# Softmax sums in fewer matmuls: two steps' exponentials added on VectorE, the last keys' products and sums in quarters of the array, sums' transfers on other queues

## The chip, the cores and the metric

The kernel runs on one core of a Trainium2 chip. The metric is the device time of one execution in microseconds (us). Three runs of the kernel before took 581.74, 581.37 and 588.43 us, a median of 581.74 us.

## The reference

Attention with capped scores over 24 heads (2 batches of 12), 448 queries and 448 keys a head, head dimension 64, followed by two feed-forward layers on the 896 x 768 result. All is float32.

```
scores = cap * tanh((q @ k.T / 8) / cap)
attn   = exp(scores - max) / (sum(exp(scores - max)) + 1e-9)
x      = attn @ v                                # 24 x 448 x 64 -> 896 x 768
h      = x @ w_in1;  y = (h * cos(h)) @ w_out1   # 768 -> 2048 -> 768
h      = y @ w_in2;  o = (h * sigmoid(h)) @ w_out2
```

The kernel leaves out the maximum (the cap bounds the scores), and divides after the product with v.

## The kernel before, in words

**The attention stage** works on pairs of heads, p = 0 to 11. The 448 keys of a head are three full chunks of 128 and a rest of 64. One pair's exponentials are the tile e32 of [128 keys, 7, 448 queries]: chunk 2t+u is step t of head u, and chunk 6 holds the two rests, head 0 in partitions 0 to 63 and head 1 in 64 to 127.

- `S_pe` makes the transposed scores of a step: for t = 0 to 2 with three matmuls a head on rounded high and low parts (float32r), head 0 on rows 0 to 63 of the array and head 1 on rows 64 to 127; step 3 in plain float32, two matmuls of 64 columns each. `S_tanh` and `S_exp` on ScalarE follow.
- `PV` multiplies with v into the bank po: rows 0 to 63 of po are head 0, 64 to 127 head 1. A matmul has all 128 keys and 64 columns, so two stand side by side in the array. For the rests v is padded with zeros to 128 keys. These are 8 matmuls a pair.
- `PV_sums` multiplies a block of ones with each chunk into the bank sm, in four column quarters of 32 (two quarters a head, to be added later): 8 matmuls a pair. A float32 matmul shows as two records in the trace.
- `evac`, `evac_sums` (VectorE) copy po and sm out. Four small transfers on SP's queue spread the rows of sums over 32 partitions, `recip` adds the two quarters and inverts, a transfer to DRAM (rs) and two back (rb) broadcast the result, `norm_mul` and `norm_split` make the high and low part of x.

The order on every engine is that of the program text (a manual schedule). Turn p of the loop issues the scores, tanh and exponentials of pair p+1, then `recip` of p-2, `qk_split` of p+2 (high and low parts of q and k), a few steps that prepare the first three weight blocks (the table `early`: w_guard and w_hi on ScalarE, w_floor, w_bits and w_lo on VectorE, w_load on POOL's queue), normalisation of p-3, the products and the sums of p and their copies. The banks po and sm are single. In the last turn the sums stand ahead of the products. The queue of SP carries vf (the loads of v), sums, rs and rb; POOL's queue carries raw (q and k, from pair 3 on) and some weights.

**The layers behind it** are matmuls against weights that are split on the way (lines 486 to 606). The first, `gemm_in`, begins with two column blocks on batch 0 (36 matmuls), four of six row blocks of batch 1 (24), and then the last two row blocks of batch 1 (24), which are pairs 10 and 11.

Of the kernel before, what the change touches and what calls it, by code (L numbers as in the profile page):

```python
# [28 lines left out]
F32 = mybir.dt.float32  # L29
# [4 lines left out]
ALU = mybir.AluOpType  # L34
# [3 lines left out]
def tile_attention_ffn_ffn(  # L38
# [10 lines left out]
    nc = tc.nc  # L49
    B, H, S, D = shape  # L50
    DM = out.shape[1]
    DFF = w_in1.shape[0] * 128
    P = 128
# [10 lines left out]
    const = ctx.enter_context(tc.tile_pool(name="const", bufs=1))  # L64
# [94 lines left out]
    with ExitStack() as actx:  # L159
        dpool = actx.enter_context(tc.tile_pool(name="dr", bufs=2, space=bass.MemoryType.DRAM))  # L160
        ap_ = actx.enter_context(tc.tile_pool(name="att", bufs=2))
        ps_s = actx.enter_context(tc.tile_pool(name="ps_s", bufs=3, space=PSUM))
        ps_o = actx.enter_context(tc.tile_pool(name="ps_o", bufs=1, space=PSUM))
        NPT = NHEAD // 2
        NCH = 7
        NV = NCH + 1
# [11 lines left out]
        ones = const.tile([P, 3, Q], F32, name="ones")  # L178

        def v_init():  # L180
            nc.gpsimd.memset(ones[:, 0], 1.0)
            for u in range(2):
                for h in range(2):
                    nc.gpsimd.memset(ones[h * D:(h + 1) * D, 1 + u], float(u == h))

# [14 lines left out]
        def load_v(p):  # L200
            if p >= NPT:
                return
            vf[p] = ap_.tile([P, NV, D], F32, tag="vf", name=f"vf{p}", bufs=2)
            nc.sync.dma_start(vf[p].rearrange("p c d -> p (c d)"), qkv[p][:, PAD + QK:])

        qh, ql = {}, {}

        def qk_split(p, part=slice(0, FULL)):
            if p >= NPT:
                return  # L210
            if p not in qh:
# [39 lines left out]

        po_, sm_ = {}, {}


        def PV(p, steps):
            first = p not in po_
            if first:
                po_[p] = ps_o.tile([P, 512], F32, tag="po", name=f"po{p}")[:, :S]
            for n, t in enumerate(steps):
                for c in range(0, P, W):  # L260
                    u, f = divmod(c, D)
                    nc.tensor.matmul(po_[p][c:c + W], vf[p][:, 2 * t + u, f:f + W], e32[p][:, min(2 * t + u, NCH - 1), :],  # L262
                                     start=first and n == 0, stop=t == 3)


        def PV_sums(p, steps):
            first = p not in sm_
            if first:
                sm_[p] = ps_o.tile([P, 512], F32, tag="sm", name=f"sm{p}")[:, :S]
            for n, t in enumerate(steps):  # L270
                for c in range(4):
                    u, x = divmod(c, 2)
                    chunk = 4 * t + 2 * x + u
                    one = ones[:, 0] if chunk < NCH - 1 else ones[:, 1 + u]
                    nc.tensor.matmul(sm_[p][c * Q:(c + 1) * Q], one, e32[p][:, min(chunk, NCH - 1), :], start=first and n == 0, stop=t == 1)  # L275

        xu, sums, rb = {}, {}, {}

        def evac(p):
            xu[p] = ap2.tile([P, S], F32, tag="xu", name=f"xu{p}", bufs=4)  # L280
            nc.vector.tensor_copy(xu[p], po_.pop(p))

        def evac_sums(p):
            x = ap2.tile([P, S], F32, tag="xs", name=f"xs{p}", bufs=2)
            sums[p] = ap2.tile([32, 2, S // 16], F32, tag="sums", name=f"sums{p}", bufs=2)
            nc.vector.tensor_copy(x[:3 * Q + 1], sm_.pop(p)[:3 * Q + 1])
            for u in range(2):
                for y in range(2):
                    at = u * D + y * Q
                    nc.sync.dma_start(sums[p][16 * u:16 * u + 16, y], x[at:at + 1])  # L290

        def recip(p):
            if p < 0:
                return
            s = sums.pop(p)
            nc.vector.tensor_tensor(out=s[:, 0], in0=s[:, 0], in1=s[:, 1], op=ALU.add)
            nc.vector.reciprocal(out=s[:, 0], in_=s[:, 0])
            d = dpool.tile([2, S], F32, tag="rs", name=f"rs{p}")
            nc.sync.dma_start(d.rearrange("h (a n) -> (h a) n", a=16), s[:, 0])
            r = ap2.tile([P, S], F32, tag="rb", name=f"rb{p}", bufs=4)  # L300
            for u in range(2):
                nc.sync.dma_start(r[u * D:(u + 1) * D, :], d[u:u + 1].to_broadcast([D, S]))  # L302
# [18 lines left out]
        def warm_up(n, ps):  # L321
            for _ in range(n):
                nc.tensor.matmul(ps, zero[:, :P], zero, start=True, stop=True)


        early = {}
        for w, turn in ((0, 2), (1, 4), (2, 6)):
            for at, *step in ((0, w_guard, w, None), (1, w_floor, w, nc.vector), (1, w_bits, w, 0), (2, w_bits, w, 1), (2, w_bits, w, 2),
                              (2, w_load, w + 2, nc.gpsimd), (3, w_hi, w), (4, w_lo, w)):
                early.setdefault(turn + at, []).append(step)  # L330
        early.setdefault(NPT - 2, []).append((w_guard, 3, None))
        early.setdefault(NPT - 1, []).append((w_floor, 3, nc.gpsimd))
# [20 lines left out]
                S_exp(0, slice(0, 4))  # L353
        S_exp(0, slice(4, NCH))
        qk_split(1)
        warm_up(4, ps_o.tile([P, 512], F32, tag="sm", name="warm1")[:, :S])
        PV(0, [0, 1])
        PV_sums(0, [0])
        for p in range(NPT):
            load(p + 3)  # L360
            if p > 0:
                load_v(p + 1)
            for t in range(3):
                S_pe(p + 1, t)
                S_tanh(p + 1, t)
            S_pe(p + 1, 3)
            S_tanh(p + 1, 3)
            S_exp(p + 1)
            recip(p - 2)
            qk_split(p + 2)  # L370
            for f, *a in early.get(p, []):
                f(*a)
            if p == NPT - 1:
                recip(p - 1)
            norm_mul(p - 3)
            norm_split(p - 3)
            if p == NPT - 1:
                PV_sums(p, [0, 1])
# [272 lines left out]
```

## Time and profile before

| | |
|---|---|
| Median of three runs | 581.74 us |
| Profiled execution, its own time | 580.33 us |
| Its span, first to last instruction | 578.5 us |
| TensorE busy | 567.1 us (98%) |
| VectorE, ScalarE, GpSimd busy | 379.9, 265.1, 155.7 us |
| Granted TensorE clock, mean | 0.997 |

The span is what lies between the first and the last instruction; the execution's time has 1.8 us around it. PE is TensorE's matmuls, DVE VectorE, ACT ScalarE, POOL GpSimd, SP the engine that only issues transfers. An L with a number is a line of the kernel before. A matmul's shown duration includes its way through the array, so that the start of one to the start of the next says what it costs. "[0.70 <-ACT e L244]" behind a row is the time that the engine stood idle ahead of it, and who ended that.

### The profile page before, as it was taken

What the parts mean: (1) busy time and instruction counts of PE and PEld (TensorE: products, weight loads), DVE (VectorE), ACT (ScalarE), POOL (GpSimd) and SP (SyncE); (2) the same over time, 40 slices, a digit from 0 to 9 for tenths busy, and PEclk for the clock granted to TensorE, in tenths of its full rate; (3) what the DMA queues carried; (4) which work ended last, traced back from release to release, by engine and by line L of the source; (5) the groups of instructions that cost most, each with busy time, mean ns of one, the idle gap of its engine ahead of it and who ended that gap; (6) DMA issues with size and microseconds to landing.
All of it is one profiled execution on the core that took longest, in us unless ns stands there. A gap on an engine that the chain in (4) does not pass through costs nothing.

```text
span 578.5 us, 7770 instructions
## 1 busy us (share of the span) xinstructions
PE 567.1 (98%) x3060; PEld 486.7 (84%) x3060; DVE 379.9 (66%) x490; ACT 265.1 (46%) x307; POOL 155.7 (27%) x84
## 2 busy tenths in 40 slices
PE   8999999889999999999999999999999999999997
PEld 4444443779999999999999999999999999999997
DVE  3356885489998888667646552888877866644501
ACT  6989985167777766233323222433333323232201
POOL 1001101033444433242332221344222223313300
PEclk9999999989999999999999999999999999999999
DMA  7245642123333323343433330343333334443102
GB/s 282 88 123 175 185 133 71 48 78 104 132 126 109 110 92 101 101 145 93 134 110 108 109 127 30 114 148 121 109 110 109 110 110 137 136 141 121 53 1 95
DMA packets 18755, 65.51 MB, mean 113 GB/s; under 512 B 4192, under 2 KB 7776, under 8 KB 18720
## 3 DMA queue, kind: packets, MB, share of 16 engines
q1 hardware_dynamic: 17280, 57.95, 31.1%
q0 software_dynamic: 1152, 6.78, 3.4%
q8 instruction: 24, 0.39, 0.3%
q10 hardware_dynamic: 288, 0.30, 0.2%
q14 instruction: 11, 0.09, 0.0%
HBM read 62.14 MB, written 2.80 MB: 112 GB/s over the span
## 4 chain that ended last, share of the span: by engine, by line
PE 88%; DMA 6%; DVE 2%; ACT 2%; SPq 1%; issue 0%; DVEq 0%
PE h L419 38%; PE o L566 20%; PE y L419 20%; PE po L262 4%; PE sc L232 2%; DMA rs<-sums 2%; DMA rb<-rs 2%; PE sm L275 2%; PE sc L236 1%; ACT e L244 1%; ACT e L250 1%; DMA raw<-in_qkv 1%; SPq L290 1%; SPq L302 1%; DMA sums<-xs 0%
## 5 line engine op out<-in xcount | busy, mean ns | idle before, releaser
L120 POOL TENSOR_SCALAR w<-w 128x768 f32<-128x768 f32 (+1 forms) x63 | 148.2, 2352 | 315.5 <-ACT w L114 251.4
L419 PE MATMUL h<-x,whi 128*128 128x448 f32 x768 | 219.6, 367 | 3.9 <-DVE x L315 3.7
L419 PEld LDWEIGHTS h<-x,whi 128*128 128x128 f32 x768 | 145.0, 189 | 16.9 <-DVE x L315 4.0
L419 PE MATMUL h<-x,wlo 128*128 128x448 f32 x384 | 140.9, 367 | 0.0
L144 ACT ACTIVATE whi<-w 128x768 fp32r<-128x768 f32 (+1 forms) x66 | 54.3, 823 | 144.0 <-DVE w L136 133.4
L566 PE MATMUL o<-whi,g 128*128 128x384 f32 x448 | 114.3, 335 | 0.0
L419 PE MATMUL y<-g,whi 128*128 128x448 f32 x384 | 109.2, 366 | 0.0
L133 DVE SCALAR_TENSOR_TENSOR w<-w,wraw 128x768 int32<-128x768 int32 (+1 forms) x66 | 61.6, 933 | 43.5 <-POOL w L120 42.5
L151 DVE TENSOR_TENSOR wlo<-w,whi 128x768 fp32r<-128x768 f32 (+1 forms) x66 | 61.4, 931 | 31.7 <-ACT whi L144 30.9
L566 PEld LDWEIGHTS o<-whi,g 128*128 128x128 f32 x448 | 81.0, 188 | 0.0
L419 PEld LDWEIGHTS h<-x,wlo 128*128 128x128 f32 x384 | 72.6, 189 | 5.7
L419 PEld LDWEIGHTS y<-g,whi 128*128 128x128 f32 x384 | 72.1, 188 | 5.9
L566 PE MATMUL o<-wlo,g 128*128 128x384 f32 x224 | 75.1, 335 | 0.0
L419 PE MATMUL y<-g,wlo 128*128 128x448 f32 x192 | 70.2, 366 | 0.0
L136 DVE SCALAR_TENSOR_TENSOR w<-wraw,w 128x768 uint32<-128x768 uint32 (+1 forms) x66 | 61.6, 934 | 2.3
L131 DVE TENSOR_SCALAR wraw<-wraw 128x768 int32<-128x768 int32 (+1 forms) x66 | 56.0, 849 | 9.7 <-ACT w L114 9.7
L114 ACT ACTIVATE w<-wraw 128x768 f32<-128x768 f32 (+1 forms) x66 | 58.0, 879 | 3.4 <-DMA wraw<-in_moe_w_out 3.4
L244 ACT ACTIVATE e<-sc,scap 128x896 f32<-128x896 f32 (+1 forms) x48 | 40.0, 913 | 12.1 <-PE sc L232 12.1
L566 PEld LDWEIGHTS o<-wlo,g 128*128 128x128 f32 x224 | 42.0, 188 | 0.0
L475 ACT ACTIVATE r<-h 128x896 f32<-128x896 f32 (+1 forms) x18 | 14.8, 835 | 58.7 <-PE h L419 56.8
L262 PE MATMUL po<-e,vf 128*64 128x448 f32 x192 | 38.5, 541 | 0.7 <-ACT e L250 0.5
L419 PEld LDWEIGHTS y<-g,wlo 128*128 128x128 f32 x192 | 36.1, 188 | 3.0
(54 smaller groups left out, 398.4 us busy)
## 6 DMA issues: line engine op xcount, KB each, us to landing
wraw<-in_moe_w_in SPq DMA_DIRECT2D x29, 768.0 KB, 4.3
wraw<-in_moe_w_out SPq DMA_DIRECT2D x22, 768.0 KB, 4.3
wraw<-in_moe_w_out SPq DMA_DIRECT2D x12, 640.0 KB, 4.0
raw<-in_qkv POOLq DMA_DIRECT2D x9, 480.0 KB, 4.5
vf<-in_qkv SPq DMA_DIRECT2D x12, 256.0 KB, 3.3
rb<-rs SPq DMA_DIRECT2D x24, 112.0 KB, 2.9
out<-os SPq DMA_DIRECT2D x13, 192.0 KB, 1.9
wraw<-in_moe_w_in POOLq DMA_DIRECT2D x3, 768.0 KB, 5.2
```

Of the source, the lines that this page charges most:

```text
L114: nc.scalar.activation(out=w32[i][:, :n, :].bitcast(F32), in_=wraw[i][:, :n, :, 1].bitcast(F32), func=AF.Abs, scale=2.0 ** -48)
L120: eng.tensor_scalar(out=t, in0=t, scalar1=2.0 ** -63, scalar2=None, op0=ALU.max)
L131: nc.vector.tensor_scalar(out=w1, in0=w1, scalar1=-0x80000000, scalar2=None, op0=ALU.bitwise_and)
L133: nc.vector.scalar_tensor_tensor(out=t, in0=t, scalar=3, in1=w1, op0=ALU.logical_shift_left, op1=ALU.bitwise_or)
L136: nc.vector.scalar_tensor_tensor(out=t, in0=w0.bitcast(U32), scalar=29, in1=t, op0=ALU.logical_shift_right, op1=ALU.bitwise_or)
L144: nc.scalar.activation(out=whi[i][:, :n, :], in_=w32[i][:, :n, :].bitcast(F32), func=AF.Copy)
L151: nc.vector.tensor_tensor(out=wlo[i][:, :n, :], in0=w32.pop(i)[:, :n, :].bitcast(F32), in1=whi[i][:, :n, :].bitcast(F32), op=ALU.subtract)
L244: nc.scalar.activation(out=e32[p][:, 2 * t:2 * t + n, :], in_=sc.pop((p, t))[:, :n, :S], func=AF.Tanh, scale=scap)
L262: nc.tensor.matmul(po_[p][c:c + W], vf[p][:, 2 * t + u, f:f + W], e32[p][:, min(2 * t + u, NCH - 1), :], start=first and n == 0, stop=t == 3)
L419: nc.tensor.matmul(pt, l, r, start=first and m == 0, stop=last and m == len(ops) - 1)
L475: nc.scalar.activation(out=r, in_=h, func=AF.Silu)
L566: nc.tensor.matmul(pt[t], l, r[:, cols], start=k == 0 and m == 0, stop=k == KF - 1 and m == 2)
```

## The change

Six matmuls of `PV` (steps 0 to 2) stay as they are. The rests, step 3, go to a new function `PV_mixed`: four matmuls of 64 keys by 64 columns, each in a quarter of the array, two of them products into po, two of them sums into sm, so v needs no padding. `PV_sums` keeps four matmuls of 32 columns: VectorE first adds the exponentials of step 0 and step 1 of both heads (`e_add`, [128, 2, 448]), and these two blocks and the two of step 2 are summed. The heads' sums now lie crosswise in sm, which rb puts right. The sums go out in two transfers on POOL's queue, v from pair 2 on too; for the last pair sums, rs and rb are on ScalarE's queue. In the last turn `recip(10)` stands behind the products, the last pair's sm lies in a bank pair of the scores, and the steps of `early` are spread over one more turn.

```diff
-            vf[p] = ap_.tile([P, NV, D], F32, tag="vf", name=f"vf{p}", bufs=2)
-            nc.sync.dma_start(vf[p].rearrange("p c d -> p (c d)"), qkv[p][:, PAD + QK:])
+            vf[p] = ap_.tile([P, NCH, D], F32, tag="vf", name=f"vf{p}", bufs=2)
+            (nc.gpsimd if p > 1 else nc.sync).dma_start(vf[p].rearrange("p c d -> p (c d)"), qkv[p][:, PAD + QK:])
...
+        def acc(d, p, tag):
+            if p in d:
+                return d[p], False
+            t = ps_o.tile([P, 512], F32, tag=tag, name=f"{tag}{p}") if p < NPT - 1 or tag == "po" else ps_s.tile([P, 2, 512], F32, tag="sc", name=f"{tag}{p}")[:, 0]
+            d[p] = t[:, :S]
+            return d[p], True
...
+        def PV(p, steps, last=False):
+            po, first = acc(po_, p, "po")
             for n, t in enumerate(steps):
...
+                for u in range(2):
+                    nc.tensor.matmul(po[u * D:(u + 1) * D], vf[p][:, 2 * t + u, :], e32[p][:, 2 * t + u, :],
+                                     start=first and n == 0, stop=last and n == len(steps) - 1)
...
+        def PV_mixed(p, last=False):
+            po, first = acc(po_, p, "po")
+            sm, _ = acc(sm_, p, "sm")
+            for u in range(2):
+                rows, other = slice(u * D, (u + 1) * D), slice((1 - u) * D, (2 - u) * D)
+                e = e32[p][rows, NCH - 1, :]
+                nc.tensor.matmul(po[rows], vf[p][rows, NCH - 1, :], e, start=first, stop=last)
+                nc.tensor.matmul(sm[other], ones[rows, Q:], e, start=True, stop=False)
...
+        def PV_sums(p):
+            sm, _ = acc(sm_, p, "sm")
+            x = e01.pop(p)
+            for c, e in enumerate((x[:, 1], e32[p][:, 5, :], x[:, 0], e32[p][:, 4, :])):
+                nc.tensor.matmul(sm[c * Q:(c + 1) * Q], ones[:, :Q], e, start=False, stop=True)
...
+        def e_add(p):
+            if p >= NPT:
+                return
+            e01[p] = ap_.tile([P, 2, S], F32, tag="e01", name=f"e01_{p}", bufs=2)
+            nc.vector.tensor_tensor(out=e01[p], in0=e32[p][:, 0:2, :], in1=e32[p][:, 2:4, :], op=ALU.add)
...
-            for u in range(2):
-                for y in range(2):
-                    at = u * D + y * Q
-                    nc.sync.dma_start(sums[p][16 * u:16 * u + 16, y], x[at:at + 1])
+            for y in range(2):
+                (nc.gpsimd if p < NPT - 1 else nc.scalar).dma_start(sums[p][:, y], x[y * Q:y * Q + D + 1:D])
...
+            eng = nc.sync if p < NPT - 1 else nc.scalar
+            eng.dma_start(d.rearrange("h (a n) -> (h a) n", a=16), s[:, 0])
...
+                eng.dma_start(r[u * D:(u + 1) * D, :], d[1 - u:2 - u].to_broadcast([D, S]))
...
-        for w, turn in ((0, 2), (1, 4), (2, 6)):
-            for at, *step in ((0, w_guard, w, None), (1, w_floor, w, nc.vector), (1, w_bits, w, 0), (2, w_bits, w, 1), (2, w_bits, w, 2),
-                              (2, w_load, w + 2, nc.gpsimd), (3, w_hi, w), (4, w_lo, w)):
+        for w, turn in ((0, 1), (1, 4), (2, 6)):
+            for at, *step in ((0, w_guard, w, None), (1, w_floor, w, nc.vector), (1, w_bits, w, 0), (2, w_bits, w, 1), (3, w_bits, w, 2),
+                              (3, w_load, w + 2, nc.gpsimd), (4, w_hi, w), (5, w_lo, w)):
...
+        e_add(0)
         warm_up(4, ps_o.tile([P, 512], F32, tag="sm", name="warm1")[:, :S])
         PV(0, [0, 1])
-        PV_sums(0, [0])
...
             recip(p - 2)
+            if p > 0:
+                e_add(p)
             qk_split(p + 2)
...
-            if p == NPT - 1:
-                recip(p - 1)
             norm_mul(p - 3)
             norm_split(p - 3)
...
+            if p < NPT - 1:
+                PV(p, [0, 1, 2] if p else [2])
+                PV_mixed(p, True)
+                evac(p)
+                PV_sums(p)
                 evac_sums(p)
-            PV(p, range(4) if p else [2, 3])
-            evac(p)
-            if p < NPT - 1:
-                PV_sums(p, [0, 1] if p else [1])
+            else:
+                PV_mixed(p)
+                PV_sums(p)
                 evac_sums(p)
+                PV(p, [0, 1, 2], True)
+                evac(p)
+        recip(NPT - 2)
```

What TensorE has from the last scores of pair 2 to the first of pair 3, before (po1 and sm1 are the banks of pair 1, xN the count of equal instructions; each float32 one shows as two records):

```order
L232 MATMUL sc2_2_260<-qh2_218,ql2_219 128x448 x2
L236 MATMUL sc2_3_268<-raw2_128 64x448 x2
L262 MATMUL po1_277<-e32_1_195,vf1_130 64x448 x8
L275 MATMUL sm1_288<-e32_1_195,ones_94 32x448 x8
L232 MATMUL sc3_0_308<-qh3_273 128x448 x2
```

and with the change (its own line numbers: 263 is `PV`, 273 and 274 `PV_mixed`, 281 `PV_sums`):

```order
L233 MATMUL sc2_3_263<-raw2_125 64x448 x2
L263 MATMUL po1_276<-e32_1_189,vf1_127 64x448 x6
L273 MATMUL po1_276<-e32_1_189,vf1_127 64x448
L274 MATMUL sm1_283<-e32_1_189,ones_94 64x448
L273 MATMUL po1_276<-e32_1_189,vf1_127 64x448
L274 MATMUL sm1_283<-e32_1_189,ones_94 64x448
L281 MATMUL sm1_283<-e01_1_268,ones_94 32x448
L281 MATMUL sm1_283<-e32_1_189,ones_94 32x448
L281 MATMUL sm1_283<-e01_1_268,ones_94 32x448
L281 MATMUL sm1_283<-e32_1_189,ones_94 32x448
L229 MATMUL sc3_0_303<-qh3_270 128x448 x2
```

Sixteen matmuls behind the scores have become fourteen: two and eight of the old ones are gone, four of 64 x 64 and four of 32 columns have come.

VectorE in the last turn, before (xu, xs are the copies of po and sm, L296 and L297 are `recip`, L308 `norm_mul`):

```order
L281 COPY xu10_988<-po10_979 128x448
L286 COPY xs10_999<-sm10_990 97x448
L296 TENSOR_TENSOR sums9_927<-sums9_927 32x28
L297 RECIPROCAL sums9_927<-sums9_927 32x28
L296 TENSOR_TENSOR sums10_1000<-sums10_1000 32x28
L297 RECIPROCAL sums10_1000<-sums10_1000 32x28
L308 TENSOR_TENSOR rb8_969<-xu8_840,rb8_969 128x448
L315 CAST x2_1_73<-rb8_969 128x448
L316 TENSOR_TENSOR x2_1_73<-rb8_969,x2_1_73 128x448
L286 COPY xs11_1033<-sm11_1024 97x448
```

and with the change:

```order
L300 COPY xs10_974<-sm10_963 97x448
L308 TENSOR_TENSOR sums9_904<-sums9_904 32x28
L309 RECIPROCAL sums9_904<-sums9_904 32x28
L289 TENSOR_TENSOR e01_11_986<-e32_11_917 128x896
L151 TENSOR_TENSOR wlo2_988<-w32_2_650,whi2_949 128x768
L321 TENSOR_TENSOR rb8_944<-xu8_821,rb8_944 128x448
L328 CAST x2_1_73<-rb8_944 128x448
L329 TENSOR_TENSOR x2_1_73<-rb8_944,x2_1_73 128x448
L300 COPY xs11_1004<-sm11_995 97x448
L295 COPY xu11_1015<-po11_994 128x448
L308 TENSOR_TENSOR sums10_975<-sums10_975 32x28
L309 RECIPROCAL sums10_975<-sums10_975 32x28
```

The reciprocal of pair 10 has moved from ahead of the copy xs of pair 11 to behind it; the sum e01 of pair 11 and a weight's step stand ahead of that copy.

SP's queue in turns 3 and 4, before:

```order
L290 DMA sums3_449<-xs3_448 16x1x28 x4
L204 DMA vf5_457<-in_qkv 128x512
L299 DMA rs2_491<-sums2_372 32x28
L302 DMA rb2_493<-rs2_491 64x448 x2
L290 DMA sums4_530<-xs4_529 16x1x28 x4
```

and POOL's queue in turns 3 and 4 with the change:

```order
L201 DMA vf4_373<-in_qkv 128x448
L302 DMA sums3_441<-xs3_440 32x1x28 x2
L194 DMA raw7_445<-in_qkv 128x960
L201 DMA vf5_447<-in_qkv 128x448
L102 DMA wraw2_493<-in_moe_w_in 128x1536
L302 DMA sums4_519<-xs4_518 32x1x28 x2
L194 DMA raw8_523<-in_qkv 128x960
```

SP keeps rs and rb alone; on POOL's queue raw and vf now stand behind the sums of the turn before.

## Rows read from the trace of the kernel before

**Rows 1.** Windows: stretch, length, busy us (instructions) by engine, PEclk, DMA share, GB/s

```profile
26.40:87.80 61.40, 61.24 (x438) 27.63 (x434) 44.33 (x81) 54.28 (x46) 5.01 (x9) 1.00 0.48 146
...
117.80:121.60 3.80, 3.61 (x10) 2.99 (x10) 3.77 (x6) 2.18 (x4) 0.15 (x1) 0.56 0.00 0
121.60:578.50 456.90, 453.21 (x2329) 427.96 (x2327) 308.32 (x357) 178.66 (x231) 145.92 (x62) 1.00 0.33 108
```

**Rows 2.** Timeline of TensorE, one pair: start, duration, line, names, shape [idle before]

```profile
26.42 0.47 PE L232 MATMUL sc<-qh 64*128 64x448 f32 x2
...
28.46 0.97 PE L236 MATMUL sc<-raw 128*64 128x448 f32 x4
29.27 3.18 PE L262 MATMUL po<-e,vf 128*64 128x448 f32 x16
32.37 1.71 PE L275 MATMUL sm<-e,ones 128*32 128x448 f32 x16
34.01 0.48 PE L232 MATMUL sc<-qh 64*128 64x448 f32 x2
...
87.78 0.47 PE L232 MATMUL sc<-qh 64*128 64x448 f32 x2
```

**Rows 3.** Groups by shape, 0 to 190 us: busy us, mean ns | idle

```profile
L438 DVE TENSOR_TENSOR g<-r,g 128x896 fp32r<-128x896 f32 x7 | 7.6, 1084 | 0.0
```

**Rows 4.** Timeline of VectorE, one turn without a wait

```profile
59.67 0.61 DVE L286 COPY xs<-sm 97x448 f32<-97x448 f32 x1
...
60.65 0.52 DVE L215 CAST qh<-raw 128x832 fp32r<-128x832 f32 x1
...
62.14 0.95 DVE L151 TENSOR_TENSOR wlo<-w,whi 128x768 fp32r<-128x768 f32 x1
...
64.91 0.62 DVE L308 TENSOR_TENSOR rb<-xu,rb 128x448 f32<-128x448 f32 x1
...
66.59 0.62 DVE L281 COPY xu<-po 128x448 f32<-128x448 f32 x1
```

**Rows 5.** Timeline of ScalarE, one pair with a weight's step

```profile
27.34 3.33 ACT L244 ACTIVATE e<-sc,scap 128x896 f32<-128x896 f32 x4 [1.26 <-PE sc L232]
...
33.52 0.90 ACT L114 ACTIVATE w<-wraw 128x768 f32<-128x768 f32 x1
34.94 3.33 ACT L244 ACTIVATE e<-sc,scap 128x896 f32<-128x896 f32 x4 [0.52 <-PE sc L232]
```

**Rows 6.** Timelines of TensorE and then ScalarE, the first pairs

```profile
11.85 0.96 PE L275 MATMUL sm<-e,ones 128*32 128x448 f32 x8
...
20.87 0.97 PE L236 MATMUL sc<-raw 128*64 128x448 f32 x4 [0.70 <-ACT e L244]
...
13.65 3.33 ACT L244 ACTIVATE e<-sc,scap 128x896 f32<-128x896 f32 x4 [0.65 <-PE sc L232]
```

**Rows 7.** Groups of transfers, 26 to 88 us: issuer, count, KB each, median us to landing

```profile
raw<-in_qkv POOLq DMA_DIRECT2D x6, 480.0 KB, 5.1
...
sums<-xs SPq DMA_DIRECT2D x32, 1.8 KB, 2.1
```

**Rows 8.** Timeline of TensorE, start of the first layer

```profile
101.06 0.67 PE L419 MATMUL h<-x,whi 128*128 128x448 f32 x2
...
113.33 0.58 PE L419 MATMUL h<-x,whi 128*128 128x448 f32 x2
...
117.78 0.47 PE L419 MATMUL h<-x,whi 128*128 128x448 f32 x1 [3.67 <-DVE x L315]
...
121.60 0.60 PE L419 MATMUL h<-x,whi 128*128 128x448 f32 x2
```

**Rows 9.** Chain of waits, pair 11's normalisation: start us, us, what

```profile
108.49 2.62 DMA sums<-xs
...
111.85 1.31 DMA rs<-sums
...
113.70 2.88 DMA rb<-rs
```

More of the change, by code (lines that the diff above doesn't have):

```diff
@@ L165, in tile_attention_ffn_ffn @@
         NCH = 7
-        NV = NCH + 1
         Q = 32
@@ L175, in tile_attention_ffn_ffn @@
         raw, vf = {}, {}
-        ones = const.tile([P, 3, Q], F32, name="ones")
+        ones = const.tile([P, 3 * Q], F32, name="ones")
         def v_init():
-            nc.gpsimd.memset(ones[:, 0], 1.0)
-            for u in range(2):
-                for h in range(2):
-                    nc.gpsimd.memset(ones[h * D:(h + 1) * D, 1 + u], float(u == h))
+            nc.gpsimd.memset(ones[:, :2 * Q], 1.0)
+            nc.gpsimd.memset(ones[:, 2 * Q:], 0.0)
         def load(p):
@@ L252, in tile_attention_ffn_ffn @@
         po_, sm_ = {}, {}
[L255 to L258, printed above, removed]
-            for n, t in enumerate(steps):
[L260 to L263, printed above, removed]
@@ L266, in PV_sums @@
[L266 to L275, printed above, removed]
+        def acc(d, p, tag):
[4 more added lines that the diff above has]
+            return d[p], True
@@ new lines, in PV_sums @@
+        def PV_sums(p):
[3 more added lines that the diff above has]
+                nc.tensor.matmul(sm[c * Q:(c + 1) * Q], ones[:, :Q], e, start=False, stop=True)
+        e01 = {}
+        def e_add(p):
[3 more added lines that the diff above has]
+            nc.vector.tensor_tensor(out=e01[p], in0=e32[p][:, 0:2, :], in1=e32[p][:, 2:4, :], op=ALU.add)
@@ L286, in evac_sums @@
             nc.vector.tensor_copy(x[:3 * Q + 1], sm_.pop(p)[:3 * Q + 1])
-            for u in range(2):
-                for y in range(2):
-                    at = u * D + y * Q
-                    nc.sync.dma_start(sums[p][16 * u:16 * u + 16, y], x[at:at + 1])
+            for y in range(2):
+                (nc.gpsimd if p < NPT - 1 else nc.scalar).dma_start(sums[p][:, y], x[y * Q:y * Q + D + 1:D])
         def recip(p):
@@ L298, in recip @@
             d = dpool.tile([2, S], F32, tag="rs", name=f"rs{p}")
-            nc.sync.dma_start(d.rearrange("h (a n) -> (h a) n", a=16), s[:, 0])
+            eng = nc.sync if p < NPT - 1 else nc.scalar
+            eng.dma_start(d.rearrange("h (a n) -> (h a) n", a=16), s[:, 0])
             r = ap2.tile([P, S], F32, tag="rb", name=f"rb{p}", bufs=4)
             for u in range(2):
-                nc.sync.dma_start(r[u * D:(u + 1) * D, :], d[u:u + 1].to_broadcast([D, S]))
+                eng.dma_start(r[u * D:(u + 1) * D, :], d[1 - u:2 - u].to_broadcast([D, S]))
             rb[p] = r
@@ L372, in tile_attention_ffn_ffn @@
                 f(*a)
-            if p == NPT - 1:
-                recip(p - 1)
             norm_mul(p - 3)
             norm_split(p - 3)
-            if p == NPT - 1:
-                PV_sums(p, [0, 1])
+            if p < NPT - 1:
[3 more added lines that the diff above has]
+                PV_sums(p)
                 evac_sums(p)
-            PV(p, range(4) if p else [2, 3])
-            evac(p)
-            if p < NPT - 1:
-                PV_sums(p, [0, 1] if p else [1])
+            else:
+                PV_mixed(p)
+                PV_sums(p)
                 evac_sums(p)
+                PV(p, [0, 1, 2], True)
+                evac(p)
+        recip(NPT - 2)
         norm_mul(NPT - 3)
@@ L626 @@
     v = np.asarray(inputs["v"]).reshape(n, 2, S, D)
-    qkv = np.zeros((n, P, pad + S + full + 128 + 8 * D), np.float32)
+    qkv = np.zeros((n, P, pad + S + full + 128 + 7 * D), np.float32)
     qkv[:, :, 0] = inputs["cap"]
@@ L636 @@
             qkv[:, :, at:at + D] = v[:, u, c * 128:(c + 1) * 128]
-        at = pad + S + full + 128 + (6 + u) * D
-        qkv[:, u * 64:(u + 1) * 64, at:at + D] = v[:, u, full:]
+        qkv[:, u * 64:(u + 1) * 64, -D:] = v[:, u, full:]
     give("qkv", qkv)
```

## The prediction

> **What bounds the kernel now.** I read the windows first. Through eight turns of the attention stage TensorE is busy 61.24 of 61.40 us at the full clock, ScalarE 54.28 and VectorE 44.33; behind 121.60 us it is busy 453.21 of 456.90 [rows 1]. So TensorE bounds both, and what shortens its own list moves the end. Behind 121.60 us the change alters nothing but the moment of the start. Everything hangs on that moment.
>
> Then the timeline of TensorE, where the start of one group to the start of the next is its price. One pair: 18 score matmuls in 2.04 us (26.42 to 28.46), the last scores 0.81, the products 3.10, the sums 1.64 and so round again, 7.59 in all [rows 2]. From 26.42 to 87.78 there are eight such rounds, 7.67 each, some of them with short waits [rows 2]. The products are 16 records in 3.10 us, two in step: eight steps of 0.376 us and 0.09 us over. The sums are 16 records in 1.64, four in step: four steps, and 0.13 over [rows 2]. The score matmuls, heads on different rows, go two in step too: nine steps in 2.04 us [rows 2]. What is over I read as the price of changing from one shape of matmul to the next, about 0.1 us.
>
> Last the end of the stage. The first layer starts at 101.06 and does 60 matmuls up to 113.33, 0.2045 each; it then lacks pair 11 until 117.78 (3.67 us idle) and goes on at 0.56 of the clock, that is at the lower level of 1.2 GHz for most of the stretch, until 121.60 [rows 1, 8]. The reader sees there a second cost, apart from TensorE's list: the chain sums, rs, rb of the last pair [rows 9].
>
> **The change part by part.**
>
> TensorE's list for a pair. Products: six matmuls, six steps: 6 x 0.376 = 2.26, 0.10 for the change of shape: 2.36. Mixed: eight records. If all four quarters go in step, two steps: 0.75, with the change 0.85. Sums: four matmuls, two steps: 0.75 and 0.13 = 0.88. With the scores 2.85 [rows 2] the round is 6.94 us where it was 7.59. The price of the mixed part is not in the trace, since no matmul there has both half the rows and half the columns. The bounds: 0.75 where four are in step, as the sums are; 1.50 where only two are, as products and scores are; 3.01 where all eight records go singly. I take 0.75, because the quarters differ from one another in rows or in columns, and either difference alone is enough to run in step in these rows.
>
> ScalarE. A pair costs it 33.52 - 27.34 = 6.18 us, and 0.90 more in six of the turns; in such a turn it idled 0.52 of 7.6 us [rows 5]. At 6.94 it is level with TensorE in those turns. I charge 0.4 us in all for the rounds between 26 and 88 us.
>
> VectorE. `e_add` is a sum of 896 float32 columns: 1.08 us by the nearest row, a subtraction of the same size [rows 3]; not under 0.52, the cast of 832 columns with one input [rows 4]. I take 1.08. A turn: xs and `recip` 0.98, `e_add` 1.08, q and k 1.49, normalisation 1.68, xu 0.62: 5.85 us [rows 3, 4]. Three weight steps took 2.77 [rows 4], and with the new table turns 6, 7 and 9 hold about two of that size each, 1.85: 7.7 us against 6.94. VectorE falls behind by 0.76 three times, at most 2.0 us together. What waits for it is the bank po of the next pair, and there is room: the mixed part ends 0.9 ahead of the turn's end, the next products begin 2.85 behind it, so 3.7 us less 0.6 for the copy. The sum that `e_add` makes is due 6.0 us into the turn and made at 2.1, or at 4.1 with the lag. I cost VectorE at nothing, with TensorE's scores as its cover. If the cover goes, 0.76 us in each of three turns, 2.3 us.
>
> Queues. Sums and vf leave SP, where rs stood behind them. POOL's raw now waits for the sums' copy of the turn before, and two more transfers: 0.62 for the copy and twice the 0.54 between rs and rb [rows 9], 1.7 us into the turn, or 3.2 with most of the lag. It landed in 5.1 us there [rows 7], and vf behind it is due 9.8 us into the turn (6.94 and the scores). That leaves 1.5 us or more: nothing. Sums needed 2.1 us on SP [rows 7]; on POOL's queue they may take as long as a raw load, 5.1, and are read a turn later: nothing.
>
> Start. `PV_sums(0, [0])` at 11.85 us goes [rows 6], so pair 1's scores begin there and ScalarE's idle 0.65 ahead of its row at 13.65 goes [rows 6]: its tanh of pair 2, 6.18 later, begins at 19.2. The score step that waited for it until 20.87 [rows 6] begins at 20.25, and 0.81 + 2.36 + 0.85 + 0.88 = 4.90 later, at 25.1, pair 3's scores, which began at 26.42: 1.3 us.
>
> Eight rounds: 8 x 6.94 + 0.4 = 55.9 in place of 61.36 [rows 2]: 5.4 us. Pair 11's scores begin at 81.0.
>
> Last turn. From there to the first layer it took 101.06 - 87.78 = 13.28 us [rows 2, 8]. Now: a round 6.94 (87.95), exponentials of pair 11 ready at 81.0 + 0.92 + 6.18 = 88.1 [rows 2, 5], mixed 0.85 (89.0); then TensorE waits for `e_add(11)`, which stands behind xs(10) and `recip(9)`: 88.1 + 0.98 + 1.08 = 90.2; sums 0.88 and products 2.36 end at 93.4: 12.4 us, so 0.9 won, though 1.2 us of it is a new wait.
>
> The chain of pair 11. VectorE has a weight's step and the normalisation of pair 8 ahead of xs(11): 90.2 + 0.92 + 1.68 + 0.62 = 93.4. Sums on ScalarE's queue, an issue of 0.54 and 2.62 (as sums took [rows 9]): 96.6; normalisation of pair 9 ends about then, `recip(11)` 0.74: 97.3; rs 1.31, issue 0.54, rb 2.88 [rows 9]: 102.0; normalised by 103.7. TensorE comes to pair 11 at 93.4 + 63 x 0.2045 = 106.3. There are 2.6 us to spare, and the wait and the lower clock go. It took 121.60 - 101.06 = 20.54 us for 72 matmuls [rows 8], and takes 72 x 0.2045 = 14.7: 5.8 us won. Bounds: nothing (the chain as late as now), and 5.8.
>
> **Sum.** 1.3 + 5.4 + 0.9 + 5.8 = 13.4 us. The profiled execution took 580.33, so 566.9. That execution lies 1.4 below the median of the three runs and 1.0 below the lowest, so by those it is 568; I put 567.5.
>
> **The rivals.**
>
> *Only two quarters in step.* The two products write the same bank po from different rows; in the trace heads on different rows always write two banks. If the second product has to wait for the first, the mixed part is 1.50, 0.75 x 12 = 9.0 us are lost, and the time is 566.9 + 9.0 = 576. For it: no row shows the contrary. Against it: the two write different partitions, and the products of the two heads do so now, in step, into one bank [rows 2]. The Trainium skill, TensorEngine Tiling, "Restrictions and Gotchas", says that different row tiles cannot access one PSUM bank at the same time, and that software has to keep them apart; by that rule this rival is the outcome, and no run here shows it yet. I give it 11%.
>
> *POOL's queue comes late.* raw, vf and sums stand behind one another there, and vf has 1.5 us to spare in the turns with lag. If every transfer took 2.5 us longer than the 5.1 of raw [rows 7], TensorE would wait about 1.0 us in each of ten turns: 577. For it: more small transfers on that queue and a busier VectorE. Against it: SP's share falls as much. The Trainium skill, SBUF — State Buffer, "Who interferes with whom", says that VectorE in its two-port modes locks out GpSimd while it writes descriptors; by it a cast of q and k (0.52 us for 832 columns [rows 4], twice the pace of a subtraction [rows 3]) would hold an issue back by half a us. I give it 9%.
>
> *Slower: the quarters go one at a time.* If a matmul that changes rows and columns at once finds the array taken, the mixed part is 3.01 instead of 0.75, 12 x 2.26 = 27.1 us, and the time is 594, 2.3% above. It turns slower where the mixed part is over 0.75 + 13.4 / 12 = 1.87 us. For it: the trace has no such shape. Against it: both differences alone overlap [rows 2]. 4%.
>
> *The chain of pair 11 is late after all,* since sums, rs and rb stand on ScalarE's queue behind weights, or rb of pairs 10 and 11 meet. Each us over 2.6 is one us of wait, up to the 5.8: 570 to 572.7. 10%.
>
> **Chances and range.** The forecast as such, 564 to 569.5: 66%. The faster side is a change of over 2%, under 570.1 us against the median; about 2% is what a measurement of this kernel can tell from no change. Faster: the 66%, less 6 for waits that I cost at nothing: 60%. Same: two quarters in step, the late queue, the late chain and those 6: 36%. Slower: 4%. The range 562 to 577 takes in the rivals up to the late queue and a better start; it leaves out the quarters one at a time.
>
> **What would show it.** Right: the start of one pair's scores to the next 6.9 to 7.0 us; in the mixed part four records starting together, and four more 0.376 later; no row of TensorE with a wait of over 1 us between 26 and 88; the first layer starting at 93 to 94 us; no stretch behind it with PEclk under 1. Wrong: mixed records in pairs or singly (the rivals on quarters); po or sm waiting for VectorE's copies or for `e_add` in the middle turns (VectorE's lag); po waiting for vf (the queue); an idle row ahead of the first layer's last 21 matmuls (the chain); or a stretch behind it that no longer runs at the pace of now, which would make the shift worth less than it is.

## The result and the profile after

The changed kernel takes **566.78 us** (median of four runs, 566.71 to 567.18), the kernel before beside it 581.65 (581.37 to 588.43); the ratio is 0.972, with a 95% interval of 0.965 to 0.979. Predicted were 567.5 us in a range of 562 to 577. The profiled execution took 566.83 us with a span of 565.0, 13.5 us under that of before.

Some executions of several kernels, by its times the kernel before among them, run the matmuls behind the attention stage at a second pace that costs 6.5 us (last section), so the kernels below are compared by the moment at which their first layer starts.

Windows of the kernel after, columns as in [rows 1]: from pair 3's scores to pair 11's, on to the first layer, its 72 matmuls, and the rest.

```profile
24.92:80.75 55.83, 55.83 (x404) 24.27 (x400) 51.96 (x90) 53.45 (x46) 25.10 (x34) 1.00 0.53 159
80.75:93.45 12.70, 11.40 (x82) 4.17 (x78) 10.56 (x20) 8.00 (x8) 6.19 (x6) 1.00 0.44 117
93.45:108.15 14.70, 14.70 (x72) 13.63 (x73) 9.83 (x20) 4.81 (x8) 0.55 (x1) 1.00 0.12 34
108.15:565.00 456.85, 453.11 (x2329) 427.94 (x2327) 308.69 (x356) 178.36 (x230) 145.24 (x62) 1.00 0.34 108
```

The same four stretches were 61.36, 13.28, 20.54 and 456.90 us [rows 1, 2, 8], and they began at 26.42. So the 13.5 us are 1.50 at the start, 5.53 in eight rounds, 0.58 in the last turn, 5.84 in the first layer's first 72 matmuls, and 0.05. TensorE has no idle time in the rounds, and its clock is 1.00 in every stretch.

TensorE's timeline of one round after, columns as in [rows 2]:

```profile
24.92 0.47 PE L229 MATMUL sc<-qh 64*128 64x448 f32 x2
...
27.75 2.42 PE L263 MATMUL po<-e,vf 128*64 128x448 f32 x12
30.10 0.59 PE L273 MATMUL po<-e,vf 64*64 64x448 f32 x1
30.11 0.59 PE L274 MATMUL sm<-e,ones 64*64 64x448 f32 x1
30.11 0.59 PE L273 MATMUL po<-e,vf 64*64 64x448 f32 x1
30.12 0.59 PE L274 MATMUL sm<-e,ones 64*64 64x448 f32 x1
30.53 0.54 PE L273 MATMUL po<-e,vf 64*64 64x448 f32 x1
...
31.01 0.96 PE L281 MATMUL sm<-e,ones 128*32 128x448 f32 x8
31.90 0.47 PE L229 MATMUL sc<-qh 64*128 64x448 f32 x2
```

Four records of the mixed part start within 0.02 us, four more 0.42 behind them. From start to start the products cost 2.35 us, the mixed part 0.91, the sums 0.89, the round 6.98. In [rows 2] the round was 7.59.

The end of the stage, TensorE and then VectorE, after:

```profile
87.99 0.59 PE L273 MATMUL po<-e,vf 64*64 64x448 f32 x1 [0.19 <-ACT e L247]
...
89.93 0.96 PE L281 MATMUL sm<-e,ones 128*32 128x448 f32 x8 [0.95 <-DVE e L289]
90.82 2.48 PE L263 MATMUL po<-e,vf 128*64 128x448 f32 x12
93.45 0.68 PE L437 MATMUL h<-x,whi 128*128 128x448 f32 x2 [0.16 <-DVE xs L300]
...
106.33 0.57 PE L437 MATMUL h<-x,whi 128*128 128x448 f32 x2
```

```profile
88.86 1.02 DVE L289 TENSOR_TENSOR e<-e 128x896 f32<-128x896 f32 x1
...
92.78 0.62 DVE L300 COPY xs<-sm 97x448 f32<-97x448 f32 x1
...
102.86 0.63 DVE L321 TENSOR_TENSOR rb<-xu,rb 128x448 f32<-128x448 f32 x1 [2.00 <-DMA rb<-rs]
103.52 0.39 DVE L328 CAST x<-rb 128x448 fp32r<-128x448 f32 x1
```

TensorE now waits 0.95 us for `e_add(11)` and 0.16 us for the copy of pair 11's sums. Pair 11's high part is ready at 103.9, and the first matmul on it starts at 106.33 without a wait: 2.4 us to spare, where [rows 8] have 3.67 us of idle and 3.80 us at a clock of 0.56 [rows 1].

### The profile page after: what moved, and what is told of

Its sections match the earlier page's. It is cut to its first block, busy times and chain, and to the rows that moved or that the text cites. A ratio compares the mean times of both kernels' runs of the same rounds, so it can differ in the third digit from the quotient of the medians.

```text
span 565.0 us, 7671 instructions
## 1 busy us (share of the span) xinstructions
PE 557.1 (99%) x3012; PEld 480.8 (85%) x3012; DVE 392.2 (69%) x502; ACT 264.6 (47%) x307; POOL 180.7 (32%) x113
## 4 chain that ended last, share of the span: by engine, by line
PE 95%; ACT 2%; DVE 1%; issue 1%; DMA 1%
PE h L437 41%; PE o L584 21%; PE y L437 21%; PE po L263 4%; PE sc L229 3%; PE sc L233 2%; PE sm L281 2%; PE po L273 2%; ACT e L241 1%; DMA raw<-in_qkv 1%; ACT e L247 1%; DVE e L289 0%; DVE x L328 0%; DVE wlo L151 0%; DVE ql L213 0%
## 5 line engine op out<-in xcount | busy, mean ns | idle before, releaser
L131 DVE TENSOR_SCALAR wraw<-wraw 128x768 int32<-128x768 int32 (+1 forms) x66 | 56.7, 859 | 9.5 <-ACT w L114 9.5
L456 DVE TENSOR_TENSOR g<-r,g 128x896 fp32r<-128x896 f32 (+1 forms) x36 | 37.5, 1050 | 0.3 <-ACT g L487 0.3
```

What stands on the lines that cost most here:

```text
L131: nc.vector.tensor_scalar(out=w1, in0=w1, scalar1=-0x80000000, scalar2=None, op0=ALU.bitwise_and)
L456: nc.vector.tensor_tensor(out=gl, in0=r, in1=gh.bitcast(F32), op=ALU.subtract)
```

## The experiments

Each kernel is the changed one with the edit that its heading names; 2 and 3 put back several things at once. The diffs show the lines that matter, and "..." marks what is left out. "First layer" is the start of its first matmul in the profiled execution, "behind it" the rest of the span.

| Kernel | First layer, us | Behind it, us | Times, us (median) | Ratio to before, 95% |
|---|---|---|---|---|
| Changed kernel | 93.45 | 471.6 | 566.7–567.2 (566.8) | 0.965–0.979 |
| Again | 93.35 | 471.6 | 566.7–567.3 (567.2) | 0.963–0.980 |
| 1 two in step | 101.25 | 478.1 | 574.3–581.4 (577.7) | 0.990–1.001 |
| 2 old matmuls | 98.67 | 478.0 | 571.6–579.9 (578.1) | 0.984–0.994 |
| 3 old queues, old order | 103.03 | 472.0 | 574.6–581.7 (576.3) | 0.991–0.998 |
| 4 no sum on VectorE | 100.13 | 478.1 | 579.9–580.5 (580.0) | 0.988–0.996 |
| 5 old queues | 101.10 | 478.0 | 574.7–581.2 (575.4) | 0.979–0.996 |
| 7 products in the wait | 94.67 | 471.6 | 566.9–568.3 (567.8) | 0.965–0.979 |
| 8 sum twice | 102.71 | 471.6 | 576.1–578.0 (577.1) | 0.980–0.996 |
| 9 last pair on SP | 93.52 | 471.5 | 566.9–573.3 (567.2) | 0.966–0.981 |
| 10 old order | 94.46 | 478.0 | 567.5–574.4 (568.4) | 0.968–0.982 |
| 11 wait filled, copy first | 92.74 | 471.6 | 566.0–566.2 (566.1) | 0.963–0.975 |
| 12 old queues, two transfers | 93.45 | 471.5 | 566.7–570.4 (568.5) | 0.967–0.979 |

**1. Is the mixed part's price on the path?** The sums of step 3 go on the same rows and columns as the product; the order of the other sums and rb follow.

```diff
-                nc.tensor.matmul(sm[other], ones[rows, Q:], e, start=True, stop=False)
+                nc.tensor.matmul(sm[rows], ones[rows, Q:], e, start=True, stop=False)
...
```

> The mixed part puts each head's sums on the same rows and columns of TensorE as that head's product, in place of the other half of the columns; the number of matmuls stays. Theory (the quarters in step are worth two steps of 0.376 us a pair, and TensorE's list is the bound): in the mixed part two records start together, not four, its price goes from 0.91 to about 1.66 us, the round from 6.98 to about 7.73, and the time from 566.8 to 566.8 + 12 x 0.75, less about 0.7 that the wait for the sum of exponentials in the last turn gives back: 575 us. Rival 1 (the products of the two heads, which write one bank from different rows, hold each other up as well): four starts one behind the other, 3 us, about 583 to 593 us. Rival 2 (VectorE or the queues set the turn, TensorE has room): the wait is taken up, below 569 us.

TensorE's timeline of it, mixed part and sums of one pair:

```profile
31.18 0.98 PE L273 MATMUL po<-e,vf 64*64 64x448 f32 x4
31.98 0.93 PE L274 MATMUL sm<-e,ones 64*64 64x448 f32 x4
32.83 0.96 PE L281 MATMUL sm<-e,ones 128*32 128x448 f32 x8
33.72 0.47 PE L229 MATMUL sc<-qh 64*128 64x448 f32 x2
```

The mixed part costs 1.65 us in place of 0.91, the round 7.73. The first layer starts 7.80 later, and the quicker five of ten runs take 574.3 to 574.7: the theory. It also answers the rival on the bank po: the two heads' products, from different rows into one bank, start together here and in the changed kernel. With the second product held up, the mixed part would have cost 1.50 us, and it costs 0.91. The Trainium skill, TensorEngine Tiling (Array Packing), "Restrictions and Gotchas", says that different row tiles cannot reach one bank at once; the four starts within 0.02 us above speak against it, and the measurement decides. The Trainium skill, PSUM — Partial Sum Buffer, "PSUM bank collisions raise a hardware error", quotes the same rule, but gives as measured that two TensorE writes from different row tiles collide inside one bank's group of 32 partitions. With that the trace agrees: the two write partitions 0 to 63 and 64 to 127.

**2. What do the queues give without the new matmuls?** `PV` and `PV_sums` of the kernel before, no `e_add`. The queues, the later `recip(10)`, the place of the last pair's sm and the table `early` stay those of the changed kernel.

```diff
-                PV(p, [0, 1, 2] if p else [2])
-                PV_mixed(p, True)
+                PV(p, range(4) if p else [2, 3])
...
```

> All the matmuls of a pair as in the kernel before (16 for products, 16 for sums, padded values, no sum of exponentials on VectorE); the queues, the last turn's order of reciprocals, the early sums of pair 0 gone and the table of weight steps are those of the change. Theory (the list gives 8 rounds x 0.61, the end of the stage gives its part through the queues and the order alone): rounds of 7.6 us, but no stall and no stretch at the lower clock behind the first layer's start: 572 to 574 us. Rival (the end of the stage was won by the shorter list, not by the queues): stall and lower clock stay, 578 to 580 us.

Rounds of 7.58 us ((86.39 - 25.74) / 8), and no stall: its window of the first layer is busy throughout.

```profile
98.67:113.37 14.70, 14.70 (x73) 13.38 (x72) 8.57 (x18) 3.38 (x6) 0.00 (x0) 1.00 0.14 39
```

So the 5.8 us of the first layer come without the shorter list. The mean granted clock was 0.999 or 1.000 in all ten runs, where the kernel before, run beside them, had 0.993 to 0.997 in 27 of its 31. The four quicker runs, 571.6 to 571.8 us, lie just under the theory's range.

**3 and 5. Old queues under the new matmuls.** 5 puts four transfers of sums, rs, rb and v on SP's queue; 3 also puts `recip(10)` back.

```diff
-            for y in range(2):
-                (nc.gpsimd if p < NPT - 1 else nc.scalar).dma_start(sums[p][:, y], x[y * Q:y * Q + D + 1:D])
+            for u in range(2):
+                for y in range(2):
+                    at = u * D + y * Q
+                    nc.sync.dma_start(sums[p][16 * u:16 * u + 16, y], x[at:at + 1])
...
```

> The matmuls and the sum of exponentials of the change; sums, rs, rb and values on SP's queue as in the kernel before, four transfers of sums, and the reciprocals of pair 10 ahead of the last turn's work again. Theory (the chain of the last pair is short enough by the shorter turn alone; the queues matter little): rounds of 7.0 us, no stall, 567 to 569 us. Rival (the queues and the order of the reciprocals took the stall and the lower clock away): rounds of 7.0 us, first layer at about 94, then a stall of 2 to 4 us ahead of its last matmuls and a clock below 1.00 behind it, 571 to 574 us.

> Only the queues are as before: four transfers of sums a pair, rs, rb and values on SP's queue, also for the last pair; matmuls, the sum of exponentials and the order of the reciprocals are the changed kernel's. With the reciprocals of pair 10 ahead of the last turn's work as well it took 576.3 us, and SP's queue held a pair for 7.4 us and more (rs's landing up to 5.1, rb 1.13, sums 2.44, values 0.53, rs 0.43) against a turn of 6.98. Theory (the queue sets the turn, and VectorE and then po wait for it; the order of the reciprocals only moves the last turn): waits of 2 to 5 us for rb in the middle turns stay, 572 to 576 us. Rival (the order of the reciprocals made those waits): 566 to 569 us.

Both of my cases for 3 missed the size and the place: no stall in the first layer, but waits of TensorE in the middle turns and ahead of the layer. 5 confirms the theory formed from that. SP's own timeline in 5 (one pair), then a row of TensorE and the window of that pair:

```profile
44.80 0.43 SPq L314 DMA_DIRECT2D rs<-sums  x1
50.26 1.13 SPq L317 DMA_DIRECT2D rb<-rs  x2
51.49 2.44 SPq L304 DMA_DIRECT2D sums<-xs  x4
54.03 1.00 SPq L201 DMA_DIRECT2D vf<-in_qkv  x1
55.07 0.43 SPq L314 DMA_DIRECT2D rs<-sums  x1
```

```profile
58.29 4.17 PE L263 MATMUL po<-e,vf 128*64 128x448 f32 x12 [1.89 <-DVE xu L295]
```

```profile
53.39:64.19 10.80, 8.91 (x54) 3.23 (x50) 8.03 (x14) 7.58 (x7) 0.54 (x1) 0.84 0.42 116
```

rb cannot go before rs has landed, 5.0 us here, and the next rs stands behind sums and v. VectorE waits up to 5.4 us for rb, copies po late, and TensorE stops for 1.89 us. The products behind it take 4.17 us in place of 2.42, at a granted clock of 0.58 from 58.29 to 62.40 us, that is for most of it at the lower level of 1.2 GHz: the pair costs 10.80 us, 3.82 more than 6.98. The turn ahead of it costs 0.54 more, the other middle turns 0.03 at most. The remaining 3.2 of the 7.65 us lie behind pair 11's scores (15.93 in place of 12.70 us), where TensorE waits 1.50 us for the copy of po and 1.46 for `e_add(11)`, and its clock falls again (0.67 from 97.50 to 101.10 us).

**12. Is it the number of transfers?** As 5, with two transfers of sums.

```diff
-                (nc.gpsimd if p < NPT - 1 else nc.scalar).dma_start(sums[p][:, y], x[y * Q:y * Q + D + 1:D])
+                nc.sync.dma_start(sums[p][:, y], x[y * Q:y * Q + D + 1:D])
...
```

> As the kernel with only the queues old (101.10 - 93.45 = 7.65 us later at the first layer), but with two transfers of sums a pair on SP's queue in place of four: 1.2 us in place of 2.4. Theory (what SP's queue needs for a pair, 7.4 us and more against a turn of 6.98, is what the old queues cost): it needs 6.2 us, the waits for rb in the middle turns go or fall under 1 us in all, first layer at 94 to 96, 567 to 569.5 us (6.5 us more where the first layer runs at 206.7 ns a matmul). Rival (not the number of transfers but the one queue, in which rb stands behind sums and values that wait for a copy): waits of 4 us and more for rb stay, 573 to 576 us.

In the profiled execution the first layer starts at 93.45, as in the changed kernel: the theory, and better than it said. SP's waits from 31 to 86 us, first of 5, then of 12 (us in total, times, longest):

```profile
SPq L317 <- DMA rs<-sums: 17.6, 7, 4.9
SPq L304 <- DVE sums L311: 2.8, 3, 1.2
```

```profile
SPq L315 <- DMA rs<-sums: 17.8, 7, 4.0
SPq L302 <- DVE sums L309: 12.4, 6, 2.7
```

The landing of rs costs the same 2.5 us a pair. With issues of 0.43, 1.13, 2.44 and 0.53 a pair holds SP's queue in 5 for 7.0 us on average, against a turn of 6.98; with 0.38, 1.16, 1.17 and 0.35 in 12, for 5.6. The second rows show the room: in 12 SP waits 12.4 us for VectorE's reciprocals, in 5 only 2.8, so there a late landing is not made up. Another of 12's four runs took 566.9 us. The other two took 570.2 and 570.4 us at mean granted clocks of 0.997 and 0.996, some 3.5 us more, and what happened in them no profile shows.

**4. What is the sum on VectorE worth?** Six sums matmuls, no `e_add`.

```diff
-            x = e01.pop(p)
-            for c, e in enumerate((x[:, 1], e32[p][:, 5, :], x[:, 0], e32[p][:, 4, :])):
+            for c, n in ((0, 1), (1, 5), (2, 0), (3, 4), (0, 3), (2, 2)):
...
```

> The quarters stay, but VectorE adds no exponentials: the sums are six matmuls on four quarters of the columns instead of four, two of them in a third step. Theory (one sum on VectorE takes the place of one step or two on TensorE and nothing else): sums go from 0.89 to 1.27 (one more step) or 1.65 us (two more), the last turn loses its wait of 0.95 us for the sum: 566.8 + 12 x 0.38 - 0.95 = 570.4, or 566.8 + 12 x 0.75 - 0.95 = 575 us. Rival (VectorE's 1.02 us a turn delays the copies of po and sm or the chain of the last pair, and is paid back without it): 567 us or less.

```profile
31.73 1.70 PE L280 MATMUL sm<-e,ones 128*32 128x448 f32 x12
33.37 0.47 PE L229 MATMUL sc<-qh 64*128 64x448 f32 x2
```

The sums cost 1.64 us in place of 0.89: the two matmuls more are two records each, so two steps. The first layer starts 6.68 later, and all ten runs have the time of the slower pace. 6.68 against the 12 x 0.75 - 0.95 = 8.05 of the theory's second case: nearer to it than to the first (3.6), and against the rival. Without the quarters in step (1), or without the sum (4), the round is 7.73, above the 7.59 of before: only both together shorten it.

**8. How much room has VectorE?** `e_add` twice.

```diff
-            nc.vector.tensor_tensor(out=e01[p], ...
+            for _ in range(2):
+                nc.vector.tensor_tensor(out=e01[p], ...
```

> VectorE adds the exponentials twice into the same place, 1.02 us more a turn. Theory (VectorE's turn is 5.85 us, with weight steps 7.7, against 6.98: light turns hide it, the heavy ones fall behind by more than the room): po waits for its copy in the heavy turns, 2 to 4 us, and the last turn's wait for the sum grows by 1.0: 569 to 572 us. Rival 1 (the room behind VectorE takes it all but in the last turn): 567.8 us. Rival 2 (VectorE is level with TensorE in every turn): 12 us more, 579.

Beyond the theory's 569 to 572: the first layer starts 9.26 later. Its windows from turn 3 on, and TensorE at the end:

```profile
31.82:59.74 27.92, 27.92 (x205) 12.15 (x201) 27.17 (x44) 26.37 (x23) 10.04 (x17) 1.00 0.50 143
59.74:84.47 24.73, 22.29 (x155) 8.84 (x152) 24.22 (x40) 20.47 (x18) 7.34 (x12) 1.00 0.50 148
84.47:102.71 18.24, 13.19 (x82) 4.34 (x78) 16.11 (x26) 7.80 (x7) 5.69 (x7) 0.91 0.33 98
```

```profile
97.95 1.72 PE L281 MATMUL sm<-e,ones 128*32 128x448 f32 x8 [2.88 <-DVE e L290]
99.60 3.18 PE L263 MATMUL po<-e,vf 128*64 128x448 f32 x12
```

In four turns VectorE (27.17 of 27.92 us) still hides it. In the next three TensorE loses 3.79 us (24.73 - 3 x 6.98), and the last stretch, from pair 11's scores on, is 18.24 in place of 12.70: there VectorE's lag, the doubled sum and the lower clock come together.

**9 and 10. The last pair's queue, and the order of the reciprocals.**

```diff
-                (nc.gpsimd if p < NPT - 1 else nc.scalar).dma_start(sums[p][:, y], ...
+                (nc.gpsimd if p < NPT - 1 else nc.sync).dma_start(sums[p][:, y], ...
...
-            eng = nc.sync if p < NPT - 1 else nc.scalar
+            eng = nc.sync
```

```diff
+            if p == NPT - 1:
+                recip(p - 1)
             norm_mul(p - 3)
...
-        recip(NPT - 2)
```

> Only the last pair's sums, rs and rb go back from ScalarE's queue to SP's, where rs and rb of pair 10 stand too. Theory (pair 11 has 2.4 us to spare, and behind rb of pair 10 it loses 1.5 to 2.5 of them): first layer as before at 93.4, pair 11 ready at 105.5 to 106.5, a wait of at most 0.5 us: 566.8 to 567.5 us. Rival (the place on ScalarE's queue is what removed the stall): a stall of 2 us or more ahead of the last 9 matmuls of the first layer, a clock under 1.00 behind it, 569 to 573 us.

> Only the order on VectorE in the last turn: the reciprocals of pair 10 stand ahead of pair 8's normalisation again, so that VectorE waits there for the sums of pair 10 to land. Theory: they land at about 91.5, VectorE loses 0.9 to 1.5 us ahead of the copy of pair 11's sums, the first layer starts that much later, and pair 11's 2.4 us to spare take up the rest: 567.7 to 568.4 us, no stall. Rival 1 (no effect): 566.8. Rival 2 (this order is what made the stall): a stall of over 1 us ahead of the last matmuls of the first layer, 570 us or more.

9 (the first diff) starts the first layer at 93.52 and has no wait behind it. Pair 11's high part is ready at 104.3, 0.4 us later than in the changed kernel and not 1.5 to 2.5. 10 (the second) starts it at 94.46, with VectorE waiting for the sums where expected, and TensorE for the copy, but none behind it either:

```profile
91.51 0.18 DVE L308 TENSOR_TENSOR sums<-sums 32x28 f32<-32x28 f32 x1 [0.55 <-DMA sums<-xs]
```

```profile
94.46 0.67 PE L438 MATMUL h<-x,whi 128*128 128x448 f32 x2 [0.93 <-DVE xs L300]
```

Both theories hold in the time, 9's not in the size of the delay. Neither edit, taken back by itself, brings the stall.

**7 and 11. Filling the new wait.** 7 puts step 0 of pair 11's products ahead of its sums; 11 also copies these sums ahead of pair 8's normalisation. The diff is the second part of 11's:

```diff
                 PV_mixed(p)
+                PV(p, [0])
                 PV_sums(p)
                 evac_sums(p)
-                PV(p, [0, 1, 2], True)
+                norm_mul(p - 3)
+                norm_split(p - 3)
+                PV(p, [1, 2], True)
...
```

> In the last turn the first products of pair 11 (two matmuls, two steps of 0.376 us) are put between the mixed part and the sums, where TensorE waits 0.95 us for the sum of exponentials. Theory (what is done in that wait is taken off the end): the first layer starts 0.75 us earlier at most, less 0.1 for one more change of shape: 566.1 to 566.3 us. Rival (the sum of exponentials or the copy of the sums is late all the same, or the first layer waits for the copies of the sums anyway): 566.8 us.

> As the kernel with the first products of pair 11 in TensorE's wait (there the first layer started 12.70 us behind pair 11's scores, as in the changed kernel, since it then waited 0.91 us for the copy of the sums), and in the last turn VectorE copies the sums of pair 11 ahead of pair 8's normalisation. Theory (both together take the wait off the end): the first layer 11.8 to 12.0 us behind pair 11's scores, in place of 12.70, and 566.0 us against 566.8. Rival (the wait moves once more, to the copy of po or to pair 8): 12.5 to 12.7 us, 566.8.

In 7 the wait only moves: 12.70 us from pair 11's scores (81.97) to the first layer, as before, since the layer then waits for the copy. In 11 it goes: 11.72 us (from 81.02).

```profile
94.67 0.68 PE L438 MATMUL h<-x,whi 128*128 128x448 f32 x2 [0.91 <-DVE xs L300]
```

```profile
92.74 0.67 PE L440 MATMUL h<-x,whi 128*128 128x448 f32 x2
```

11 takes 566.1 us, the quickest of all, 0.7 to 1.1 us under the changed kernel's medians; the two were timed in different groups of runs, so the trace's 0.98 us is the better evidence.

**The changed kernel again.**

> The changed kernel itself once more, beside the others. Behind the first layer's start, the profiles so far show two paces for the same matmuls of 448 columns, both at a granted clock of 1.00: 202.7 ns from start to start in the changed kernel, the kernel before and the one with the old queues, 206.7 ns in the other three; 1,728 of them make 6.5 us or so. Theory A (which pace an execution gets is chance, the same for all kernels): some of these runs lie at 566.8 and some at 573.3 us. Theory B (what comes ahead of the first layer decides, and the changed kernel gets the quick one): all at 566.8 us.

All four runs lie at 566.7 to 567.3 us. Beside the ten runs of 4, all at the slower pace, that speaks against theory A. Theory B does not hold strictly either: 1, 2, 5, 9 and 10 had both paces by their times, each with nothing changed between its runs.

## Why the prediction was right, and where it was not

- **TensorE's list: right.** 6.98 for 6.94, mixed 0.91 for 0.85, sums 0.89 for 0.88, products 2.35 for 2.36. Four quarters in step was the choice on which most hung; experiment 1 prices the other at 7.8 us (9.0 in the rival). ScalarE's 0.4 us did not come. In all 13.4 us were forecast, and 13.5 came.
- **Start and last turn: right in sum.** 1.50 for 1.3; 0.58 for 0.9, since TensorE's wait for `e_add(11)` is 0.95 for 1.2, but the first layer waits 0.16 for the copy of the sums, and the shapes change more often. 11 shows that the wait was on the path.
- **"Queues ... nothing": right for the new queues, reasoned with a gap.** TensorE has no wait for a transfer in the attention stage from 26 us on. But I weighed what POOL's queue gets and never what SP's had needed: about 7.0 us a pair against the new turn of 6.98. Left as they were, the queues cost 7.65 us (5), more than half of the gain; with two transfers fewer a pair nothing of it is left in two of four runs (12). The forecast held because the change had made the edit whose need I did not see, and that was luck.
- **VectorE at nothing: right, with less room than I gave.** No row shows a wait of TensorE for it between 26 and 80 us. 8 puts 1.02 us a turn more at 9.3 us.
- **Stall and lower clock, 5.8: right in size (5.84), the reason left out.** The chain of pair 11 ran nearly as laid out (its high part ready at 103.9 for 103.7), but what had made it late before I did not work out. In the kernel before, first VectorE and then SP's queue show it:

```profile
101.00 0.18 DVE L296 TENSOR_TENSOR sums<-sums 32x28 f32<-32x28 f32 x1 [3.86 <-DMA sums<-xs]
...
103.02 0.62 DVE L286 COPY xs<-sm 97x448 f32<-97x448 f32 x1
```

```profile
105.46 1.08 SPq L302 DMA_DIRECT2D rb<-rs  x2
106.59 2.49 SPq L290 DMA_DIRECT2D sums<-xs  x4
```

  With `recip(10)` early, VectorE waits 3.86 us for pair 10's sums and copies pair 11's only at 103.02, and their transfers stand behind rb of pair 10 until 106.59. By these profiles a long wait takes both the early `recip(10)` and the old queues. With the early order alone VectorE waits 0.55 us there (10), with the old queues alone not at all for sums (5), with both 2.36 (3). In 3 the lateness shows ahead of the layer, which now waits for that copy, where the kernel before started it 1.96 us ahead of the copy:

```profile
103.03 0.68 PE L440 MATMUL h<-x,whi 128*128 128x448 f32 x2 [2.48 <-DVE xs L300]
```

  So 9 and 10 each took back one thing while the other still helped. 5 is a weaker witness, since its own waits had moved the layer's start by 7.65 us. The stall is not in every execution of the kernel before either: four of the 31 runs beside 1 to 4 took 575.6 to 577.4 us at a granted clock of 1.000, the others 580.1 us and more at 0.997 and less; no profile shows the four. The kernel before with one of the two edits and nothing else was not run, so the share of each stays open.
- **POOL's queue late, slower by single quarters: did not come.** No wait of po for v or raw, no record of the mixed part alone. An issue on POOL was held up for 0.34 us at most: two of nine issues of v between 26 and 88 us, at 28.28 and 49.22, took 0.92 us in place of 0.58, both beside a weight's step of VectorE (L131) that started meanwhile.

## What to carry to other kernels

When an engine's turn gets shorter, add up each queue's turn as well: issues and the landings that stand in it, not only the engines' busy time. A queue that was just hidden becomes the bound, and through an engine that waits for its transfers it stops the one you made faster. A wait filled at one place is won only when what is waited for next is early too, so move both. Where two edits can each remove the same wait, taking back one of them shows nothing: take back both (3) beside each alone.

## What the runs showed of the hardware

Behind the attention stage the same matmuls of 448 columns have one of two paces for a whole execution, both at a granted clock of 1.00. Two rows of TensorE's timeline, 97 groups of three matmuls apart, after:

```profile
129.84 0.36 PE L437 MATMUL h<-x,wlo 128*128 128x448 f32 x1
...
188.81 0.36 PE L437 MATMUL h<-x,wlo 128*128 128x448 f32 x1
```

and in experiment 1:

```profile
129.66 0.37 PE L437 MATMUL h<-x,wlo 128*128 128x448 f32 x1
...
189.80 0.37 PE L437 MATMUL h<-x,wlo 128*128 128x448 f32 x1
```

That is 202.7 and 206.7 ns from start to start. The spans behind the first layer's start fall at 471.5 to 472.0 or at 478.0 to 478.1 us, with nothing between; the kernel before has 477.4, with its 5.84 us of stall and lower clock in it. By their times, 1 and 2 had both paces in ten runs, 4 the slower in all ten, the changed kernel the quicker in all eight. 9, which reaches the layer within 0.1 us of the changed kernel, has one run of four at 573.3 us. The kernel before took 586 us and more, the slower pace by its times, in 16 of 31 runs beside 1 to 4, which ran on one chip, and in 4 of 14 beside the others, on two more; so the chip may have a part in it. The start of the layer, a wait ahead of it or its lack do not sort the profiles. What decides it stays open.
